# A state-space block with two mixers: u's second DFT and the transform back on mirrored rows, in 64x64 tiles

## Chip, cores, metric

One core of a Trainium2 chip runs the whole program in one launch. The metric is device time in microseconds (us) of that launch; lower is better. PE is the matmul engine, DVE the vector engine, ACT the scalar engine, POOL the general one, SP the engine that only issues DMAs and waits. Everything below is float32; a float32 matmul is two PE instructions in the trace, so counts of PE instructions there are twice the counts in the code.

## The reference

Shapes: A_u is [1, 2048, 512], the state has 128 complex modes for each of 512 channels.

```python
mod = (_silu(c) @ w_mod).reshape(c.shape[0], 6, 1, -1)
h = _layernorm(x) * (1 + ca) + sa
# _A_ref: K[d, l] = Re sum_n C[d,n] exp(dt A[d,n] l) dt B[d,n]; y = causal convolution of h with K
Kf = rfft(pad(K, 2L)); Uf = rfft(pad(h^T, 2L)); y = irfft(Uf * Kf)[:L] + h * Dskip
x = x + ga * y
h = _layernorm(x) * (1 + cb) + sb
x = x + gb * _B_ref(h)      # two LayerNorm/gelu mixers: shift by 1 and 2 rows between w1 and w2, then w3, w4
```

The part that changes is the convolution: the second step of the Fourier transform of `h` (called u here), the product with the spectrum of K, and the transform back.

## The kernel before

The program runs in three stages.

**Stage one (0 to 208 us).** It builds K by exponentials and sines, 32 rounds of `turns`, `products` and `burst`. Between the rounds it normalises u and does u's first DFT: a row number is 64q + b (q below 32, b below 64), and `u_dft` transforms over q by matmuls from 32 rows to 64 columns of the array (`FU`). Its results go out to DRAM (`VU`, by `evict`, one 64-partition DMA for each half of a tile).

**Stage two (208 to 322 us).** `k_first` (8 rounds) does the first DFT of K into `VK`. Then comes a loop of 16 steps: a step is a half of the channels (`jh`, 2) and four of the 32 first frequencies (`kc`, 8). A step has four parts:

- `spectrum_k` (line 669): second DFT of K over b, from `VK`, 32 matmuls with 64 rows and 64 columns each; result in two PSUM banks `pk2`.
- `multiply` (lines 680, 681, 685): on DVE, four products of 512 elements a partition and four sums and differences of 256; result `zc`.
- `back` (line 695): the first half of the inverse over `Gm`, 64 rows by 128 columns, real and imaginary part added up in PSUM (`pz`); ACT copies it to `z`, and POOL sends `z` to DRAM (`ZT`, line 701), 128 partitions of 4 KB.
- `spectrum_u` (line 646): second DFT of u over b and over real and imaginary part, 128 rows by 64 columns, with the weights `T2`; ACT copies the result to `us` in six pieces of 256.

The order in every engine's queue is the program's (`tc.manual_schedule()`): step n issues `spectrum_k(n)`, `multiply(n)`, `back(n-1)`, `spectrum_u(n+1)`, and then the loads. So PE runs K(n), back(n-1), U(n+1), K(n+1), and so on. `z`, `us` and `zc` have two buffers each: the copy into `z` of step n waits until the store of step n-2 has landed. `block` tiles (`ldp`, seven buffers) hold what SP loads: u's spectrum for step n+3, parts of w1, and what the second half of the inverse reads. SP's DMAs go out in program order, each waiting for the eighth before it to land; in steps 3, 4, 6 and 8 four DMAs each bring back the raw u (`load_x`, line 714, 32 partitions of 8 KB each, rows 128 KB apart in DRAM) for the residual.

The second half of the inverse, over k1 (`inv_half`, line 724), reads `ZT` back as [128, 4, 256] tiles (`load_inv`, line 709) and adds to the residual `X2` (line 727). It runs in eight groups (two channel halves by four groups g of four columns in each quarter). The first channel half's loads stand in the loop behind step 9 (g = 0), 13 and 14; its groups 0 and 1 are computed in the loop, groups 2 and 3 behind it. The second half's groups 3 and 0 come first behind the loop, since the mixers start from them.

**Stage three (322 to 705 us).** The two mixers, with weights split in a high and a low part (`three`, `chan`). The change does not touch them.

Of the kernel before, what the change touches and what calls it, by code (L numbers as in the profile page):

```python
# [21 lines left out]
JB = (1, 0, 2, 3)  # L22
# [5 lines left out]
def shape_constants():  # L28
# [5 lines left out]
    FU = np.zeros((4, 32, 2, 2, 2, 32))  # L34
    for h in range(2):
        for cp2 in range(2):
            cp = 2 * h + cp2
            FU[1 - cp if cp < 2 else cp, :, h, cp2] = W
    FU = FU.reshape(128, 2, 2, 2, 32).transpose(0, 1, 2, 4, 3)
# [6 lines left out]
    T3 = np.stack([s, -s]).reshape(128, 32 * 64)  # L46
    h, cq, cp2 = np.meshgrid(np.arange(2), np.arange(16), np.arange(2), indexing='ij')
    b = c2b((2 * h + cp2) * 16 + cq).reshape(64)
    al = 2 * np.pi * b[None, :] * k2[:, None] / 64
    c, s = np.cos(al), np.sin(al)  # L50
    Gm = np.zeros((64, 2, 64, 2))
    Gm[:, 0, :, 0], Gm[:, 0, :, 1], Gm[:, 1, :, 0], Gm[:, 1, :, 1] = c, s, -s, c
    Gm = np.tile(Gm.reshape(64, 256), (2, 1))
    FI = np.zeros((2, 2, 32, 16, 2, 2, 32))
    for hh in range(2):
        for c2 in range(2):
            for cc in range(16):
                bb = int(c2b(np.array((2 * hh + c2) * 16 + cc)))
                th = 2 * np.pi * (k1[:, None] + .5) * (bb + 64 * q[None]) / 4096
                FI[c2, 0, :, cc, hh, bb // 16 - 2 * hh] = np.cos(th) * (2 / 4096)  # L60
                FI[c2, 1, :, cc, hh, bb // 16 - 2 * hh] = -np.sin(th) * (2 / 4096)
# [19 lines left out]
    for e in range(16):  # L81
# [8 lines left out]
        FU=FU.reshape(128, 256), FK=FK.reshape(128, 128), T2=T2, T3=T3, G=Gm,  # L90
        FI=FI.reshape(128, 16 * 128), C0=C0, C1=C1, CE=CE, PA=PA.reshape(128, 512), PB=PB.reshape(128, 2048), ID=np.eye(128)).items()}


def layouts(inp):
    a = lambda n: np.asarray(inp[n])
    perm = lambda x: np.ascontiguousarray(x.reshape(4, 32, 4, -1).transpose(1, 0, 2, 3).reshape(512, -1))
    m = {"u": a("A_u")[0], "wm": a("w_mod"), "c": np.ascontiguousarray(a("c").reshape(4, 128).T),
         "ld": np.ascontiguousarray(perm(a("A_log_dt")).reshape(4, 128).T),
         "dk": a("A_Dskip").reshape(4, 128),
# [12 lines left out]
def body(ctx, tc, A):  # L112
# [76 lines left out]
    FU = ph.tile([128, 2, 128], F32, name="FU")  # L189
# [237 lines left out]
    def u_dft(b, cp2):  # L427
        x = ut[b // 4]
        ps = [psu.tile([128, 512], F32, name="pu") for h in range(2)]
        for i in range(2):  # L430
            for h in range(2):
                q = 64 * (1 - i if h == 0 else i)
                j = slice(32 * JB[2 * h + cp2], 32 * JB[2 * h + cp2] + 32)
                T.matmul(ps[h][q:q + 64], FU[j, h, cp2 * 64:cp2 * 64 + 64], x[j, b % 4 + i],  # L434
                         start=True, stop=True, skip_group_check=True)

        def evict():
            vs = uv.tile([128, 2, 512], F32, name="vs")
            for h in range(2):
                act(vs[:, h], ps[h])  # L440
                c0 = h * 32 + cp2 * 16 + (14 - b if h == 0 else b)
                for i in range(2):
                    Y.dma_start(dram(VU, (c0 + i) * 256, [[16384, 64], [1048576, 2], [1, 256]]),
                                vs[i * 64:i * 64 + 64, h].rearrange("p (a d) -> p a d", a=2))
# [158 lines left out]
    T3 = c2.tile([128, 32, 64], F32, name="T3")  # L603
    Gm = c2.tile([128, 2, 128], F32, name="Gm")
    FI = c2.tile([128, 16, 2, 64], F32, name="FI")
# [5 lines left out]
    psy = a2.enter_context(pool("psy", bufs=2, space=PSUM, side="right"))  # L611
    psa = s2x.enter_context(pool("psa", bufs=2, space=PSUM))
    BANK = ("pk1", "pk2", "pz", "py")
    block = lambda: ldp.tile([128, 4, 256], F32, name="ld")

    def k_first(r):
        ps = [(psy if n == "py" else psa).tile([128, 4, 2, 64], F32, name=n) for n in BANK]
# [20 lines left out]
    def spectrum_u(jh, kc):  # L638
        vu = vus.pop((jh, kc))
        us = s2.tile([128, 2, 3, 256], F32, name="us")  # L640
        for i in range(2):
            q = psa.tile([128, 2, 256], F32, name="pk1")
            for ro in range(2):
                for kk in range(2):
                    k1 = kc * 4 + 2 * kk + i
                    T.matmul(q[kk * 64:kk * 64 + 64, ro], T2[k1 // 16][:, k1 % 16, ro * 64:ro * 64 + 64],  # L646
                             vu[:, 2 * kk + i], start=True, stop=True, skip_group_check=True)
            for n in range(3):
                act(us[:, i, n].rearrange("p (h j g) -> p h j g", h=2, j=2),
                    q[:, n % 2].rearrange("p (j h g) -> p h j g", h=2, j=2))  # L650
        return us

    def spectrum_k(jh, kc):
        p = [psa.tile([128, 2, 2, 128], F32, name="pk2") for gh in range(2)]
        for i in range(2):
            for ro in range(2):
                for ri in range(2):
                    for kk in range(2):
                        for gh in range(2):
# [7 lines left out]
                            else:  # L667
                                w = T3[rows, k1]
# [5 lines left out]
    def multiply(jh, kc, us, p):  # L674
        zc = zcs[jh, kc] = [s2.tile([128, 2, 256], F32, name=f"zc{n}") for n in range(2)]
        m = []
        for gh in range(2):
            s = slice(gh * 128, gh * 128 + 128)
            m.append([s2.tile([128, 2, 2, 128], F32, name=n) for n in ("ma", "mb")])
            V.tensor_mul(m[gh][0], p[gh], us[:, :, :2, s])  # L680
            V.tensor_mul(m[gh][1], p[gh], us[:, :, 1:, s])
        as2 = lambda z: z.rearrange("p i (j g) -> p i j g", j=2)
# [612 lines left out]
```

## Time and profile before

| | |
|---|---|
| median of three runs | 707.08 us (704.25 to 710.23) |
| span of the profiled execution | 704.8 us; no other time is listed for it |
| PE busy | 666.8 us (95% of the span) |
| DVE, ACT, POOL busy | 500.4, 335.3 and 92.2 us |
| granted PE clock, mean | 0.996 of full speed |
| moved by DMA | 86.56 MB, mean 123 GB/s |

A page of the profile gives for each engine its busy time; a row of 40 digits, each the busy tenths of a slice of 17.6 us; then the chain of work that ended last, followed back from the last instruction, and groups of instructions with their mean duration. A matmul's duration includes its way through the array, and matmuls in different parts of the array overlap: what a group costs is read from the distance of its first and last start, not from the mean. "DMA share" in a table of stretches is the summed time of the packets over 16 DMA engines; 1.0 to 1.1 is all of them busy.

### The profile page before, as it was taken

Reading aid. Unit: us, or ns where it says so; the run is one execution under the profiler, and the core shown is the slowest. Engines: PE = TensorE matmul, PEld = TensorE weight load, DVE = VectorE, ACT = ScalarE, POOL = GpSimd, SP = SyncE. Lnnn points to the kernel's source line nnn. Section 1 sums busy time; section 2 is a strip of 40 time slices with the busy share of each in tenths; the row PEclk is TensorE's granted clock in tenths of the full one; section 3 lists DMA queues with packets and bytes.
Section 4 is the critical chain, followed back from the end, with each engine's and each line's share of the span. In section 5 each row is a group of like instructions: output and inputs, shape, how many; then the busy total and the mean of one; then the engine's idle time right before and its main releaser. Section 6 shows DMA issues by size and latency. Waiting matters only on the chain.

```text
span 704.8 us, 16806 instructions
## 1 busy us (share of the span) xinstructions
PE 666.8 (95%) x7067; PEld 516.0 (73%) x7067; DVE 500.4 (71%) x827; ACT 335.3 (48%) x553; POOL 92.2 (13%) x205
## 2 busy tenths in 40 slices
PE   1899999999999999998999899999999999999997
PEld 0456656565678565664778889899899988989896
DVE  7899999999986656778996867467455536354522
ACT  3978898888956354551443732224132221213120
POOL 4011121021100000001671101001110000000000
PEclk9999999999999999999999999999999999999999
DMA  8903274746449997885459111020110201011011
GB/s 289 285 2 93 78 210 125 181 103 189 134 125 340 233 276 266 293 278 201 144 185 301 61 31 31 16 56 21 55 36 16 66 11 39 22 30 31 1 31 31
DMA packets 56692, 86.56 MB, mean 123 GB/s; under 512 B 5541, under 2 KB 43433, under 8 KB 54921
## 3 DMA queue, kind: packets, MB, share of 16 engines
q1 hardware_dynamic: 52536, 66.87, 34.0%
q0 software_dynamic: 3200, 17.57, 7.0%
q8 instruction: 56, 0.92, 0.6%
q10 hardware_dynamic: 880, 1.05, 0.5%
q14 instruction: 20, 0.16, 0.1%
HBM read 59.25 MB, written 32.90 MB: 131 GB/s over the span
## 4 chain that ended last, share of the span: by engine, by line
PE 79%; DVE 11%; DMA 3%; ACT 3%; issue 2%; POOL 1%; SPq 0%; DVEq 0%; ACTq 0%; POOLq 0%
PE pm L834 7%; PE pm L831 7%; PE pm L832 7%; PE xx L457 7%; PE pa L947 6%; PE pa L948 6%; PE pa L955 6%; PE pk L669 4%; PE pk L646 4%; PE pz L695 4%; PE kp L507 4%; PE pu L434 2%; PE ph L886 2%; PE ph L888 2%; PE ph L885 2%; DMA w4l<-Dw 2%
## 5 line engine op out<-in xcount | busy, mean ns | idle before, releaser
L120 ACT ACTIVATE gh<-pm 128x512 fp32r<-128x512 f32 (+1 forms) x48 | 26.9, 561 | 200.7 <-PE pm L834 200.7
L831 PE MATMUL pm<-nh,w3h 128*128 128x256 f32 (+1 forms) x352 | 86.7, 281 | 2.9 <-ACT nh L120 2.9
L832 PE MATMUL pm<-nh,w3l 128*128 128x256 f32 (+1 forms) x352 | 86.3, 280 | 0.0
L939 DVE TENSOR_TENSOR gl<-gf,gh 128x512 fp32r<-128x512 f32 (+1 forms) x48 | 30.8, 642 | 68.3 <-ACT gf L120 68.3
L947 PE MATMUL pa<-w4h,gh 128*128 128x512 f32 (+1 forms) x176 | 69.5, 395 | 0.0
L831 PEld LDWEIGHTS pm<-nh,w3h 128*128 128x128 f32 (+1 forms) x352 | 66.0, 188 | 4.7 <-ACT nh L120 3.2
L948 PE MATMUL pa<-w4l,gh 128*128 128x512 f32 (+1 forms) x176 | 68.9, 391 | 0.0
L832 PEld LDWEIGHTS pm<-nh,w3l 128*128 128x128 f32 (+1 forms) x352 | 65.9, 187 | 1.8 <-DVE w3l L749 0.2
L834 PE MATMUL pm<-nl,w3h 128*128 128x256 f32 (+1 forms) x352 | 55.6, 280 | 0.0
L955 PE MATMUL pa<-w4h,gl 128*128 128x512 f32 (+1 forms) x176 | 48.0, 390 | 0.0
L834 PEld LDWEIGHTS pm<-nl,w3h 128*128 128x128 f32 (+1 forms) x352 | 47.4, 188 | 0.2 <-DVE nl L804 0.2
L758 POOL TENSOR_TENSOR rs<-mv,eps_t 128x1 f32<-128x1 f32 (+1 forms) x39 | 11.0, 282 | 278.5 <-DVE mv L764 265.9
L457 PE MATMUL xx<-MG,ON 64*128 64x512 f32 x160 | 47.0, 389 | 0.0
L458 PE MATMUL xx<-MG,ON 64*128 64x512 f32 x160 | 47.0, 389 | 0.0
L891 DVE TENSOR_TENSOR h<-h,ph 128x512 f32<-128x512 f32 x16 | 11.0, 687 | 45.4 <-PE ph L888 45.4
L475 DVE SCALAR_TENSOR_TENSOR e<-tr,p 128x512 f32<-128x512 f32 x64 | 41.1, 683 | 0.4 <-ACT tr L120 0.4
L120 ACT ACTIVATE z<-pz 128x512 f32<-128x512 f32 x32 | 17.4, 595 | 48.4 <-PE pz L695 17.1
L680 DVE TENSOR_TENSOR ma<-pk,us 128x512 f32<-128x512 f32 x32 | 21.9, 686 | 26.0 <-issue 11.8
L507 PEld LDWEIGHTS kp<-e,e 128*32 128x32 f32 x2048 | 30.1, 110 | 13.1 <-issue 7.1
L484 DVE TENSOR_TENSOR e<-tr,p 128x1024 f32<-128x1024 f32 x32 | 39.0, 1218 | 0.0
L485 DVE TENSOR_TENSOR e<-tr,m 128x1024 f32<-128x1024 f32 x32 | 39.0, 1218 | 0.0
L120 ACT ACTIVATE p<-xx 128x1024 f32<-128x1024 f32 (+1 forms) x40 | 37.5, 980 | 2.1 <-PE xx L258 0.4
(231 smaller groups left out, 1747.0 us busy)
## 6 DMA issues: line engine op xcount, KB each, us to landing
VU<-vs SPq DMA_DIRECT2D x64, 128.0 KB, 3.2
ld<-VU SPq DMA_DIRECT2D x16, 512.0 KB, 15.1
ZT<-z POOLq DMA_DIRECT2D x15, 512.0 KB, 6.9
ld<-ZT SPq DMA_DIRECT2D x12, 512.0 KB, 7.0
Dw<-in_w POOLq DMA_DIRECT2D x8, 688.0 KB, 4.8
xu<-in_u SPq DMA_DIRECT2D x16, 256.0 KB, 10.2
KX<-in_u SPq DMA_DIRECT2D x16, 256.0 KB, 13.2
GD<-go SPq DMA_DIRECT2D x16, 256.0 KB, 2.2
```

Of the source, the lines that this page charges most:

```text
L120: return S.activation(out, in_, f, bias=bias, scale=scale)
L457: T.matmul(x[:, :512], la, ma, start=(i == 0), stop=(i == len(ops) - 1))
L458: T.matmul(x[:, 512:], lb, mb, start=(i == 0), stop=(i == len(ops) - 1))
L475: V.scalar_tensor_tensor(e0[:, 1, a], tr[:, 1, 0], 1.0 - 2.0 * a, mg[:, a], op0=OP.mult, op1=OP.mult)
L484: V.tensor_mul(e0[:, 0], tr[:, 0, 0:1].to_broadcast([128, 2, 512]), mg)
L507: T.matmul(kp[32 * j:32 * j + 32, (k % 2) * 4 + g], e1[:, r, d], e0[:, r, :, d * 32:d * 32 + 32], start=(r == 0), stop=(r == 1), skip_grou ...
L831: T.matmul(p, wh[:, k, c], hi[k], start=(k == 0), stop=False)
L832: T.matmul(p, wl[:, k, c], hi[k], start=False, stop=False)
L834: T.matmul(p, wh[:, k, c], lo[k], start=False, stop=(k == 3))
L947: T.matmul(acc[i], gh[:m, e, s], W4h[:m, f], start=(f == 0), stop=False)
L948: T.matmul(acc[i], gh[:m, e, s], W4l[:m, f], start=False, stop=False)
L955: T.matmul(acc[i], gl[:m, e, s], W4h[:m, f], start=False, stop=(f == 10))
```

## The change

The block of 64 columns b is taken as 32 pairs mirrored about its middle (31 - b' and 32 + b'). `u_dft` now forms sums and differences within its matmuls: its rows hold both columns of a pair and its weights hold W and W with the order turned round and its sign. Each call makes one kind (`eo`), from 64 rows to 64 columns of the array. With them the real and the imaginary part of the second DFT need 64 rows each, so `spectrum_u` contracts over 64 rows with the new weights `TU`, and `back` gives the cosine and the sine product of each part apart (`Gm` is half as large, no adding up in PSUM). The signs of a pair's two members are then in `FI`, and `inv_half` makes 32 rows of one column at a time.

```diff
 def load_u(g):
-    for bp in range(4):
-        Y.dma_start(x[bp * 32:(bp + 1) * 32],
-                    dram(A["u"], (bp * 16 + g * 4) * 512, [[64 * 512, 32], [1, 2048]]))
+    for n, bp in enumerate(UB):                                    # UB = (1, 2, 0, 3)
+        Y.dma_start(x[n * 32:(n + 1) * 32],
+                    dram(A["u"], (bp * 16 + g * 4) * 512, [[64 * 512, 32], [1, 2048]]) if bp > 1 else
+                    dram(A["u"], (bp * 16 + 15 - g * 4) * 512, [[64 * 512, 32], [-512, 4], [1, 512]]))
 def u_dft(b, eo):
-            j = slice(32 * JB[2 * h + cp2], 32 * JB[2 * h + cp2] + 32)
-            T.matmul(ps[h][q:q + 64], FU[j, h, cp2 * 64:cp2 * 64 + 64], x[j, b % 4 + i], ...)
+            j = slice(64 * h, 64 * h + 64)
+            T.matmul(ps[h][i * 64:i * 64 + 64], FU[j, eo], x[j, b % 4 + i], ...)
-psy = a2.enter_context(pool("psy", bufs=2, space=PSUM, side="right"))
 psa = s2x.enter_context(pool("psa", bufs=2, space=PSUM))          # pk1, pz (before: pk2 too)
+psb = s2x.enter_context(pool("psb", bufs=4, space=PSUM))          # pk2: four banks instead of two
 def spectrum_u(jh, kc):
-    us = s2.tile([128, 2, 3, 256], F32, name="us")
-    for i in range(2):
-        q = psa.tile([128, 2, 256], F32, name="pk1")
-        for ro in range(2):
-            for kk in range(2):
-                k1 = kc * 4 + 2 * kk + i
-                T.matmul(q[kk * 64:kk * 64 + 64, ro], T2[k1 // 16][:, k1 % 16, ro * 64:ro * 64 + 64],
-                         vu[:, 2 * kk + i], start=True, stop=True, skip_group_check=True)
-        for n in range(3):
-            act(us[:, i, n].rearrange(...), q[:, n % 2].rearrange(...))
+    us = s2.tile([128, 3, 2, 256], F32, name="us")
+    q = [psa.tile([128, 2, 256], F32, name="pk1") for ro in range(2)]
+    for i in range(2):
+        for kk in range(2):
+            for ro in range(2):
+                r = slice(ro * 64, ro * 64 + 64)
+                T.matmul(q[ro][kk * 64:kk * 64 + 64, i], TU[r, kc * 4 + 2 * kk + i], vu[r, 2 * kk + i],
+                         start=True, stop=True, skip_group_check=True)
+    for n in range(3):
+        act(us[:, n], q[n % 2])
+def flip(kc):                       # the T3, formerly loaded by two DMAs, from T2
+    t = t3s[kc] = c2.tile([128, 8, 64], F32, name="T3", bufs=3)
+    for gh in range(2):
+        r = slice(gh * 64, gh * 64 + 64)
+        P.tensor_scalar(t[r], T2[kc // 4][r, kc % 4 * 4:kc % 4 * 4 + 8, 64 - gh * 64:128 - gh * 64], -1.0, None, op0=OP.mult)
 def multiply(jh, kc, us, p):
-    m = []
-    for gh in range(2):
-        s = slice(gh * 128, gh * 128 + 128)
-        m.append([s2.tile([128, 2, 2, 128], F32, name=n) for n in ("ma", "mb")])
-        V.tensor_mul(m[gh][0], p[gh], us[:, :, :2, s])
-        V.tensor_mul(m[gh][1], p[gh], us[:, :, 1:, s])
-    for gh in range(2):
-        for n in range(2):
-            V.tensor_tensor(zc[n]..., as2(m[gh][n][:, :, 0]), as2(m[gh][n][:, :, 1]), op=(OP.subtract, OP.add)[n])
+    m = [s2.tile([128, 2, 2, 2, 128], F32, name=n, bufs=1) for n in ("ma", "mb")]
+    for gh in range(2):
+        for n in range(2):
+            V.tensor_mul(m[n][:, gh], p[gh], us[:, n:n + 2, :, gh * 128:gh * 128 + 128].rearrange("p r i d -> p i r d"))
+    for n in range(2):
+        V.tensor_tensor(zc[n]..., m[n][:, :, :, 0], m[n][:, :, :, 1], op=(OP.subtract, OP.add)[n])
 def back(jh, kc):
-            T.matmul(o[kk], Gm[r, n], zc[n][r], start=(n == 0), stop=(n == 1))
+            T.matmul(o[kk][n * 64:n * 64 + 64], Gm[r, n], zc[n][r], start=True, stop=True, skip_group_check=True)
+    def store(q, a, b):
+        for n in range(2):
+            q.dma_start(dram(ZT[jh], n * 16384 + (kc * 4 + a) * 256, [[32768, 32], [8192, 2], [1, (b - a) * 256]]),
+                        z[n * 64:n * 64 + 64, a:b].rearrange("p k d -> p (k d)"))
-        P.dma_start(ZT[jh][:, kc * 4:kc * 4 + 4], z)
+        store(P, 0, 4)
 def inv_half(jh, g, i, pl, name):
-        for h in range(2):
-            T.matmul(p[h * 64:h * 64 + 64, e], FI[:, cc, h], zz[h][:, cc % 4], ...)
+        for bp, (c, sg) in enumerate(((31 - b, 1), (15 - b, 1), (b, 0), (16 + b, 0))):
+            T.matmul(p[bp * 32:bp * 32 + 32, e], FI[:, c, sg], zis[jh, c // 4][:, c % 4], ...)
 # in the loop
+            if n % 2 == 0 and n < 14:
+                flip(steps[n + 2][1])
-            if n == 9: load_inv(0, 0)
+            if n == 10:
+                for k in (0, 3, 4, 7): load_inv(0, k)
-            if n == 11: inverse(0, 0)
+            if n == 12: inverse(0, 0)
-            if n == 13: load_inv(0, 1); load_inv(0, 2)
-            if n == 14: load_inv(0, 3)
+            if n == 13:
+                inverse(0, 3)
+                for k in (1, 2, 5, 6): load_inv(0, k)
 # behind the loop
-    inverse(0, 2)
-    inverse(0, 3)
+    for i in range(2):
+        inv_half(0, 2, i, psy, "py")()
```

Three places show how the queues move. The first is SP's queue from step 8 of the loop on; L636 and L626 are the loads of u's spectrum, L743 and L738 those of w1 and then w2, L709 and L707 those of the inverse (`ld<-ZT`), `FI` its weights. Before:

```order
40 L743 DMA ld<-in_w 128x2x512
41 L636 DMA ld<-VU 128x4x256
42 L1127 DMA FI<-in_FI 128x2048
43 L743 DMA ld<-in_w 128x2x512
44 L709 DMA ld<-ZT_61 128x4x256 x2
45 L636 DMA ld<-VU 128x4x256 x3
46 L743 DMA w2l<-Dw_64 128x2x512 x2
47 L709 DMA ld<-ZT_61 128x4x256 x6
48 L699 DMA ZT_62<-z 128x512
```

And with the change:

```order
53 L738 DMA ld<-in_w 128x2x512
54 L626 DMA ld<-VU 128x4x256
55 L1125 DMA FI<-in_FI 128x2048
56 L738 DMA ld<-in_w 128x2x512
57 L626 DMA ld<-VU 128x4x256
58 L707 DMA ld<-ZT_61 128x4x256 x4
59 L626 DMA ld<-VU 128x4x256 x2
60 L738 DMA w2l<-Dw_64 128x2x512 x2
61 L707 DMA ld<-ZT_61 128x4x256 x4
62 L692 DMA ZT_62<-z 32x2x512 x2
```

The first loads of the inverse stand behind one more load of u's spectrum and are four instead of two; the other four (before six) follow w2.

The second place is POOL's queue in the loop: the issues of the stores of `z`, and with the change `flip` (L648) between them. Before:

```order
59 L521 DMA Dw_64<-in_w 16x8192 x2
60 L701 DMA ZT_61<-z 128x1024 x8
61 L701 DMA ZT_62<-z 128x1024 x7
62 L758 TENSOR_TENSOR rs_79<-mv_78,eps_t 128x1
```

With the change:

```order
59 L510 DMA Dw_64<-in_w 16x8192 x2
60 L648 TENSOR_SCALAR T_3093<-xu 64x512 x2
61 L648 TENSOR_SCALAR T_3368<-xu 64x512 x2
62 L692 DMA ZT_61<-z 32x2x1024 x4
63 L648 TENSOR_SCALAR T_3514<-xu 64x512 x2
64 L692 DMA ZT_61<-z 32x2x1024 x4
65 L648 TENSOR_SCALAR T_3663<-xu 64x512 x2
```

A step's store is two DMAs of 64 partitions instead of one of 128, and every second step a pair of `flip` instructions stands behind them.

The third is DVE in a step in the middle of the loop: products into `ma` and `mb`, then sums and differences into `zc`. Before:

```order
323 L680 TENSOR_TENSOR ma<-pk_3938,us 128x512
324 L681 TENSOR_TENSOR mb<-pk_3938,us 128x512
325 L680 TENSOR_TENSOR ma<-pk_3939,us 128x512
326 L681 TENSOR_TENSOR mb<-pk_3939,us 128x512
327 L685 TENSOR_TENSOR zc_3972<-ma 128x4x64
328 L685 TENSOR_TENSOR zc_3973<-mb 128x4x64
329 L685 TENSOR_TENSOR zc_3972<-ma 128x4x64
330 L685 TENSOR_TENSOR zc_3973<-mb 128x4x64
```

With the change:

```order
327 L676 TENSOR_TENSOR ma<-pk_4145,us 128x512
328 L676 TENSOR_TENSOR mb<-pk_4145,us 128x512
329 L676 TENSOR_TENSOR ma<-pk_4146,us 128x512
330 L676 TENSOR_TENSOR mb<-pk_4146,us 128x512
331 L678 TENSOR_TENSOR zc_4179<-ma 128x2x2x128
332 L678 TENSOR_TENSOR zc_4180<-mb 128x2x2x128
```

Four short instructions have become two of twice the length.

More of the change, by code (lines that the diff above doesn't have):

```diff
@@ L33, in shape_constants @@
     W = np.stack([np.cos(th), -np.sin(th)], 1)
-    FU = np.zeros((4, 32, 2, 2, 2, 32))
-    for h in range(2):
[L36 to L39, printed above, removed]
+    Wt = W.transpose(0, 2, 1)
+    FU = np.stack([np.stack([Wt, -Wt[..., ::-1]], 1), np.stack([Wt, Wt[..., ::-1]], 1)])
+    FU = np.stack([FU, FU])
     FK = np.zeros((2, 2, 32, 2, 64))
@@ L717, in inv_half @@
     def inv_half(jh, g, i, pl, name):
-        zz = zis[jh, g]
         p = pl.tile([128, 2, 256], F32, name=name)
         for e in range(2):
-            for h in range(2):
-                b = g * 4 + i * 2 + e
-                cc = 15 - b if h == 0 else b
-                T.matmul(p[h * 64:h * 64 + 64, e], FI[:, cc, h], zz[h][:, cc % 4],
+            b = g * 4 + i * 2 + e
+            for bp, (c, sg) in enumerate(((31 - b, 1), (15 - b, 1), (b, 0), (16 + b, 0))):
+                T.matmul(p[bp * 32:bp * 32 + 32, e], FI[:, c, sg], zis[jh, c // 4][:, c % 4],
                          start=True, stop=True, skip_group_check=True)
@@ L727, in inv_half, with inverse_parts @@
         return lambda: V.tensor_add(x, p, x)
-    def inverse_parts(jh, g):
-        return [inv_half(jh, g, i, psy, "py") for i in range(2)]
+    def inverse_parts(jh, g, pl, name):
+        return [inv_half(jh, g, i, pl, name) for i in range(2)]
     def inverse(jh, g):
-        for f in inverse_parts(jh, g):
+        for f in inverse_parts(jh, g, psa, "pz"):
             f()
@@ L1114, in body @@
             if n == 15:
-                i1 = inverse_parts(0, 1)
+                i1 = inverse_parts(0, 1, psb, "pk2")
             if n < 15:
@@ L1157, in body @@
         psw = ctx.enter_context(tp("psw", 2, space=PSUM))
+        psy = a2.enter_context(tp("psy", 2, space=PSUM, side="right"))
         def keep(n):
```

125 lines of the change are left out of this document (57 added, 68 removed).

## The prediction

> **What bounds the kernel now.** First the page: which engine is busy, and where.
>
> ```profile
> span 704.8 us, 16806 instructions
> ...
> PE 666.8 (95%) x7067; PEld 516.0 (73%) x7067; DVE 500.4 (71%) x827; ACT 335.3 (48%) x553; POOL 92.2 (13%) x205
> ...
> DMA  8903274746449997885459111020110201011011
> ```
>
> PE is the bound of the whole, but the change lies in stage two, slices 12 to 18, and there the DMA row reads 9998788: nearly as full as PE. So two limits have to be weighed. The chain of waits, cut to a quiet stretch of the loop, shows the first:
>
> ```profile
> 278.45 1.91 PE pk L669 x64
> 280.36 1.92 PE pz L695 x8
> 282.28 1.88 PE pk L646 x16
> 284.16 1.91 PE pk L669 x64
> ```
>
> K, back and U follow each other with no gap: a step is 284.16 - 278.45 = 5.71 us, all PE. The second limit stands in a table of four stretches of the loop:
>
> ```profile
> 224.80:273.50 48.70, 46.87 (x727) 29.14 (x729) 30.59 (x64) 21.19 (x63) 3.39 (x7) 1.00 1.06 279
> 273.50:286.00 12.50, 12.50 (x221) 7.89 (x214) 7.95 (x17) 7.65 (x23) 1.44 (x3) 1.00 0.38 132
> 286.00:310.00 24.00, 24.00 (x359) 14.72 (x359) 20.09 (x42) 12.40 (x35) 2.12 (x4) 1.00 1.02 356
> 310.00:322.40 12.40, 11.73 (x144) 6.36 (x136) 10.29 (x21) 5.94 (x14) 1.06 (x2) 1.00 0.46 156
> ```
>
> The last three columns are granted clock, DMA share and GB/s. For 72.7 of 97.6 us the sixteen DMA engines are full, at two very different rates. And the waits in the loop:
>
> ```profile
> ACT z L120 <- DMA ZT<-z: 13.2, 3, 5.7
> ...
> DVE ma L680 <- ACT us L120: 9.8, 4, 4.0
> ```
>
> Three times ACT could not overwrite `z` because the store two steps back had not landed; what stands behind it in ACT's queue (the copies to `us`) then held DVE. The DMAs already touch the chain.
>
> **The change part by part: PE.** The rows of the three matmuls, with rows by columns of the array in use and the size of one:
>
> ```profile
> L669 PE MATMUL pk<-VK,xu x768: 266/269/321, 224.8 to 316.0; 64*64 64x128 f32 x192
> L646 PE MATMUL pk<-ld,xu x256: 379/379/431, 223.0 to 314.0; 128*64 128x256 f32 x128
> ...
> L695 PE MATMUL pz<-zc,Gm x128: 589/589/693, 231.5 to 322.2; 64*128 64x512 f32 x128
> ```
>
> K streams 64 instructions of 128 columns in 1.91 us, U 16 of 256 in 1.88, back 8 of 512 in 1.92: 8192 columns and 4096 twice, in the same time, because K's quarters of the array run four at a time and the halves of the others two. The change makes U and back quarters with the same number of instructions and columns, so I give them K's rate: 0.94 and 0.96 us. A step becomes 1.91 + 0.94 + 0.96 = **3.8 us**, 1.9 less, 30 us over 16 steps. The sharing between the array's quarters is bounded by K's row (1.9 saved) and by no gain at all (0).
>
> **DVE and ACT.** One step's instructions, as starts:
>
> ```profile
> 318.35 0.68 DVE L680 TENSOR_TENSOR ma<-pk,us 128x512 f32<-128x512 f32 x1
> ...
> 319.54 0.41 DVE L685 TENSOR_TENSOR zc<-ma 128x256 f32<-128x256 f32 x1
> 319.87 0.42 DVE L685 TENSOR_TENSOR zc<-mb 128x256 f32<-128x256 f32 x1
> ...
> L120 ACT ACTIVATE us<-pk 128x256 f32<-128x256 f32 x94 | 27.8, 399 | 2.4 <-PE pk L646 2.0 <-ACT z L120 0.4
> ...
> L120 ACT ACTIVATE z<-pz 128x512 f32<-128x512 f32 x30 | 16.3, 595 | 46.0 <-PE pz L695 17.1 <-DMA ZT<-z 13.2 <-issue 10.5
> ```
>
> A product comes every (319.54 - 318.35) / 2 = 0.60 us, a short sum every 0.33: 4 x 0.60 + 4 x 0.33 = 3.7 us now, 6 x 0.60 = 3.6 with two long ones. ACT: 6 x 27.8/94 + 2 x 16.3/30 = 2.9 now, 5 x 0.54 = 2.7 then. So DVE and PE come level at 3.6 to 3.8 us; the four `pk2` banks let K(n+1) run beside multiply(n), which two banks did not allow. By the engines a step could fall to about 3.9 us.
>
> **DMA, the term that decides.** What is moved in the loop stays the same (`TU` is as large as the old `T3`). Full engines read 1.02 to 1.06, so the loop's transfers alone need (48.70 x 1.06 + 12.50 x 0.38 + 24.00 x 1.02 + 12.40 x 0.46) / 1.06 = 86.6 / 1.06 = **81.7 us**, and of 97.6 us at most 15.9 can go. Some of it stays: behind the last loads only stores are left, and there is nothing to fill about one step and a half. I take 5 us as idle (the stretch from 310 has 54% of 12.4, or 6.7 us). That leaves **-11 us** for the loop. Its ends are -16 (nothing idle) and -4 (as idle as now, 12 us).
>
> The stretch at 279 GB/s is slow by its loads of raw u, and that bears on the stores, which the change cuts in two halves of 64 partitions:
>
> ```profile
> 21.00:25.00 4.00, 3.89 (x10) 3.04 (x10) 3.96 (x4) 3.79 (x7) 0.00 (x0) 1.00 1.06 394
> 26.00:34.00 8.00, 7.35 (x46) 3.79 (x38) 5.28 (x9) 6.96 (x11) 0.00 (x0) 1.00 1.01 218
> 64.40:65.00 0.60, 0.60 (x34) 0.45 (x36) 0.60 (x2) 0.53 (x2) 0.00 (x0) 1.00 0.94 195
> ...
> ZT<-z POOLq DMA_DIRECT2D x15, 512.0 KB, 6.9
> ...
> ZT<-z POOLq DMA_DIRECT2D x1, 512.0 KB, 3.0
> ```
>
> The first stretch loads `w_mod` to 128 partitions, the second u to 32 partitions at a time, the third stores `VU` from 64: 394, 218 and 195 GB/s with the engines equally full. (Their steps in DRAM differ too, so the rows alone don't say which of the two it is.) A store of 512 KB is 1.3 us at the first rate and 2.5 at the others: the halves cost between 0 and 1.2 us more each. Stores that go out beside the u loads meet a slow queue anyway; of the eight behind them some meet 128-partition loads, which keep the engines busy while a half-store waits. I take +1 us in all, nearest to none, and keep 0 and +10 (eight stores in full) as ends. The two last rows are the median time to land, in the loop and once with nothing beside it.
>
> [...]
>
> **POOL and SP.**
>
> ```profile
> 266.63 0.37 SPq L743 DMA_DIRECT2D ld<-in_w  x1
> 283.58 0.92 SPq L709 DMA_DIRECT2D ld<-ZT  x2
> ...
> 248.98 0.53 POOL L701 DMA_DIRECT2D ZT<-z  x1 [7.88 <-ACT z L120]
> ...
> 262.13 0.53 POOL L701 DMA_DIRECT2D ZT<-z  x1 [7.93 <-ACT z L120]
> ...
> 278.03 0.53 POOL L701 DMA_DIRECT2D ZT<-z  x1 [4.16 <-ACT z L120]
> 283.74 0.53 POOL L701 DMA_DIRECT2D ZT<-z  x1 [5.17 <-ACT z L120]
> ...
> L853 POOL COPY win<-go x2: 501/502/504, 355.8 to 359.4; 128x384 f32<-128x384 f32 x2
> ```
>
> POOL issues a store in 0.53 us; two make 1.1. `flip` is new: 16 instructions of 64 x 512. The nearest row is 0.50 us for 384 elements a partition, so 0.7 each, 1.3 a pair and 11 us in all, bounded by 0 and twice that; POOL has 3.39 of 48.70 us busy, so it fits between stores. A new wait comes of it: K(n+2) waits for the flip, which stands behind the store of step n-1, whose copy waits for a landing. It has two steps' time; if that cover is gone it costs up to 2.4 us in a step.
>
> SP sat from 267.0 to 283.6 until the store of step 7 (issued 278.03) had landed, with all later loads behind it. The change puts one more load of u ahead of that wait and needs 2 MB instead of 1 before the first inverse in step 12; at the 356 GB/s above that is 3 us more on a wait that two steps cover. I take 0, the end is +4.
>
> **Stage one.** u's first DFT keeps its count and sizes:
>
> ```profile
> L434 PE MATMUL pu<-xu,FU x128: 587/613/638, 61.3 to 202.5; 32*64 32x512 f32 x128
> ...
> L147 DVE BATCH_NORM_STATS2 lus<-xu x16: 662/687/689, 39.8 to 179.0; 128x6 f32<-128x512 f32 x16
> ```
>
> It used four parts of the array before (two of rows, two of columns) and does after: 0, with ends of -1 and +1. Half of u's loads come in 2 KB pieces; the first loads are over at 34 us, u is first read at 39.8: the six us between cover them.
>
> **Behind the loop.**
>
> ```profile
> 326.39 3.68 DMA ld<-ZT
> ...
> 330.20 1.10 PE py L724 x8
> ```
>
> The first inverse of the second half waited 3.7 us for 512 KB. It now needs four tiles' halves, 1 MB: 0.5 MB at 356 GB/s is +1.5. The last `back` is 0.96 shorter, the second piece of the last store is issued 0.37 later (SP's row above): **+0.9**. The inverse's own matmuls are twice as many with half the columns of the array, four side by side for two: 0. One group of four fewer remains here, in time in which PE waited; one more is in the loop, where PE is no longer the bound.
>
> **Sum:** -11 + 1 + 0.9 = -9 against the span, 695.7. The median of the three runs stands 2.3 us above the span, so 698 is what I expect of a median.
>
> **The rivals.**
>
> *The engines are the bound (12%).* The DMA share shrinks with less competition, and DVE sets the steps.
>
> ```profile
> L749 DVE TENSOR_TENSOR w1l<-ld,w1h 128x512 fp32r<-128x512 f32 x4 | 2.6, 688 | 2.1 <-ACT w1h L120 2.1
> ```
>
> Eight steps at 3.9 are 31; the other eight 8 x 3.6 with the splits of w1 and (taken alike) w2, 2 x 2.6, and four additions of an inverse, 4 x 0.6: 37. With a last step run out, 3.8, that is 72 for 97.6, -26. Against it: a share of 1.06 for 48.7 us. Time 707 - 26, about 682.
>
> *What the loop gains is lost to late landings (33%).* Half-stores pay for the eight steps (+10), or the first inverse stalls PE (+4) and the last steps idle as now (+7). The loop ends where it did: 704 to 709, and 707 stands for it.
>
> *Slower (7%).* The half-stores pay 1.2 us each in all 15 stores, since engines that wait for one can do nothing else: 81.7 + 5 + 18 = 105 us for 97.6, +7, with the tail +8: 715. It decides from the ninth store that pays in full (81.7 + 5 + 9 x 1.2 = 97.5). For it: 195 GB/s in the one pure half-store row; against it: the loop's stores never run alone.
>
> *PE's clock drops in the new gaps (8%).* It has happened in this trace:
>
> ```profile
> 389.97 0.39 PE L831 MATMUL pm<-nh,w3h 128*128 128x256 f32 x1 [2.94 <-ACT nh L120]
> ...
> 391.30:394.80 3.50, 3.50 (x18) 3.39 (x17) 3.47 (x7) 1.18 (x4) 0.00 (x0) 0.51 0.36 111
> ```
>
> After 2.94 us of waiting PE ran 3.5 us at 0.51, a loss of 1.7 us of matmul time. Amid the u loads two steps took 262.13 - 248.98 = 13.15 us by POOL's stores, 6.6 each; of such a step PE would now wait 6.6 - 3.8 = 2.8; seven such drops are 7 x 1.7 = 12 us of PE time, a third of it perhaps on the path: +4, time 702. [...]
>
> *The quarters don't overlap (2%).* U and back then keep their time: 707. K's row speaks against it.
>
> **Numbers.** The forecast has 38%, its own range 691 to 703 (loop -16 to -4, less or more of the +1). **The range 686 to 709** leaves out the engine-bound case and the slower one. One per cent, 7 us, is about what a measurement of this kernel can tell from no change: faster than 700.0 is two thirds of the forecast, the engine-bound case and a fourth of the clock and late cases, **0.48**; slower than 714.2 **0.07**; the rest **0.45**.
>
> **What would show it.** Right: L636 and L688 (U and back) at 0.94 and 0.96 us a step; DMA share about 1.05 without the dip at 273 to 286; z's copies waiting for `ZT` landings more than 13.2 us; the loop from 225 to 310 or 312. Wrong: a share well under 1 with steps of 3.9 us (engines), stores landing 3 us later than 6.9 (halves), a clock column under 0.9 in the loop, or PE waiting for `ld<-ZT` in step 12.

## The result, and the profile after

The changed kernel took 699.33 us (median of 12 runs, 697.88 to 705.2) against 705.89 of the kernel before on the same chip (703.27 to 710.84): a ratio of 0.9922, with a 95% interval of 0.9893 to 0.9951, so 3.5 to 7.6 us faster. Its profiled execution has a span of 699.7 us, 5.1 less than before. The page's rows that answer to those of before:

```profile
span 699.7 us, 16980 instructions
...
PE 639.1 (91%) x7195; PEld 507.1 (72%) x7195; DVE 497.8 (71%) x795; ACT 331.9 (47%) x505; POOL 125.3 (18%) x236
...
DMA  8903274745539999987268111020110201011011
```

PE worked 27.7 us less and the program ended 5.1 us sooner: most of what was taken off PE turned into waiting. The table of the four stretches of the loop (busy time of PE, PE's weight loads, DVE, ACT and POOL, then granted clock, DMA share and GB/s) says where:

```profile
224.80:273.50 48.70, 35.07 (x740) 27.12 (x732) 29.77 (x49) 20.47 (x40) 17.10 (x20) 0.89 1.06 277
273.50:286.00 12.50, 10.85 (x261) 9.05 (x255) 10.59 (x19) 8.99 (x19) 6.85 (x9) 1.00 0.78 251
286.00:310.00 24.00, 20.70 (x424) 14.21 (x424) 23.21 (x41) 13.04 (x27) 10.10 (x12) 1.00 1.03 353
310.00:322.40 12.40, 7.17 (x78) 3.24 (x78) 8.55 (x17) 2.16 (x5) 1.07 (x2) 0.99 0.50 136
```

In the first stretch PE is busy for 35.07 us instead of 46.87, at the same share (1.06) and the same rate (277 for 279 GB/s). POOL's issues of stores are the loop's milestones: the first, the eighth (step 7) and the fifteenth. Of the kernel before (the eighth, 278.03, stands in the prediction), then of the changed one:

```profile
235.11 0.57 POOL L701 DMA_DIRECT2D ZT<-z  x1 [52.55 <-ACT z L120]
...
319.68 0.53 POOL L701 DMA_DIRECT2D ZT<-z  x1 [5.17 <-ACT z L120]
```

```profile
232.05 1.19 POOL L692 DMA_DIRECT2D ZT<-z  x2 [13.38 <-ACT z L110]
...
275.23 1.07 POOL L692 DMA_DIRECT2D ZT<-z  x2 [1.76 <-ACT z L110]
...
310.32 1.07 POOL L692 DMA_DIRECT2D ZT<-z  x2 [2.97 <-ACT z L110]
```

From the first store to the eighth it took 42.9 us before and 43.2 now; from the eighth to the fifteenth 41.7 before and 35.1 now. The gain at the fifteenth is 9.4 us: 3.1 stood there at the first store, none came in the seven steps amid the loads of raw u, 6.6 behind them.

The chain of waits shows a kind of wait in the first half that the kernel before hardly had (rows with start, length and what it was):

```profile
231.50 1.74 issue
...
238.03 5.68 issue
...
251.01 1.17 issue
...
257.18 2.13 issue
...
267.07 2.43 issue
...
302.04 1.91 PE pk L666 x64
303.95 0.86 PE pz L688 x8
304.81 0.86 PE pk L636 x16
```

The three last rows are K, back and U in a quiet step: 3.63 us for what took 5.71 (the next K follows at 305.67). The five others are PE in the middle of a group, waiting for no semaphore that the profile shows. What the waits add up to, and behind it PE's wait on K in the kernel before:

```profile
DVE ma L676 <- PE pk L666: 17.0, 8, 6.4
...
ACT z L110 <- DMA ZT<-z: 13.0, 3, 5.3
...
PE pk L666 <- issue: 10.7, 6, 5.7
```

```profile
PE pk L669 <- issue: 1.3, 2, 0.7
```

And behind the loop, where the last step's products lead to the last piece of the last store, and this to the loads of the inverse. Two rows of the kernel before, then the chain of the changed one:

```profile
317.15 0.68 DVE L680 TENSOR_TENSOR ma<-pk,us 128x512 f32<-128x512 f32 x1
...
323.92 0.35 ACTq L699 DMA_DIRECT2D ZT<-z  x1
```

```profile
309.30 0.60 DVE ma L676
...
316.18 2.85 DMA ZT<-z
...
319.84 4.95 DMA ld<-ZT
...
324.93 1.97 PE py L719 x16
```

The first inverse of the second half starts at 324.93 instead of 330.20, 5.3 us sooner: of the 9.4 us, 4.1 were given back in the tail. From there to the end it is 374.8 us now and 374.6 before.

### The profile page after: what moved, and what is told of

Same layout as the page of the kernel before. It is cut to its first block, busy times and chain, and to the rows that moved or that the text cites. A ratio compares the mean times of both kernels' runs of the same rounds, so it can differ in the third digit from the quotient of the medians.

```text
span 699.7 us, 16980 instructions
## 1 busy us (share of the span) xinstructions
PE 639.1 (91%) x7195; PEld 507.1 (72%) x7195; DVE 497.8 (71%) x795; ACT 331.9 (47%) x505; POOL 125.3 (18%) x236
## 3 DMA queue, kind: packets, MB, share of 16 engines
q10 hardware_dynamic: 896, 1.05, 0.6%
## 4 chain that ended last, share of the span: by engine, by line
PE 69%; DVE 17%; issue 4%; DMA 4%; ACT 3%; POOL 1%; SPq 0%; ACTq 0%; DVEq 0%; POOLq 0%
PE pm L829 7%; PE pm L827 7%; PE pm L826 7%; PE pa L950 6%; PE pa L942 6%; PE pa L943 6%; PE xx L446 6%; PE pk L666 3%; PE kp L496 3%; PE pz L688 2%; DVE e L464 2%; DVE e L474 2%; PE pk L612 2%; PE ph L881 2%; PE ph L883 2%
## 5 line engine op out<-in xcount | busy, mean ns | idle before, releaser
L666 PE MATMUL pk<-VK,xu 64*64 64x128 f32 x768 | 36.8, 274 | 10.7 <-issue 10.7
L666 PEld LDWEIGHTS pk<-VK,xu 64*64 64x64 f32 x768 | 32.7, 135 | 14.0 <-issue 13.2
L950 PEld LDWEIGHTS pa<-w4h,gl 128*128 128x128 f32 (+1 forms) x176 | 33.0, 188 | 8.3 <-DVE gl L934 1.2
```

The costliest lines, as they stand in the source:

```text
L666: T.matmul(p[gh][kk * 64:kk * 64 + 64, i, ro], w, VK[jh][rows, ri * 32 + k1].rearrange("p j g -> p (j g)"), start=(ri == 0), stop=(ri == 1 ...
L950: T.matmul(acc[i], gl[:m, e, s], W4h[:m, f], start=False, stop=(f == 10))
```

## The experiments

All are variants of the changed kernel unless said otherwise; ratios are against the kernel before, run beside them. Milestones in us from the profiled executions:

| | store 1 | store 8 | store 15 | first inverse behind | span | ratio (95%) |
|---|---|---|---|---|---|---|
| before | 235.11 | 278.03 | 319.68 | 330.20 | 704.8 | |
| changed | 232.05 | 275.23 | 310.32 | 324.93 | 699.7 | 0.9922 (0.9893 to 0.9951) |
| changed, again | 232.60 | 278.12 | 313.72 | 328.32 | 702.7 | 0.9926 (0.9906 to 0.9946) |
| old tiles | 233.95 | 276.45 | 320.93 | 334.60 | 709.3 | 1.0087 (1.0058 to 1.0116) |
| half the code of K | 232.09 | 272.01 | 307.30 | 321.57 | 696.5 | 0.9929 (0.9906 to 0.9952) |
| whole stores | 232.12 | 271.71 | 306.78 | 319.30 | 693.8 | 0.9897 (0.9865 to 0.9928) |
| no raw u | 232.72 | 261.65 | 295.93 | 310.26 | 685.7 | 0.9751 (0.9710 to 0.9792) |
| raw u to 128 partitions | 231.65 | 263.89 | 296.61 | 312.05 | 686.7 | 0.9764 (0.9742 to 0.9786) |
| before, raw u to 128 | 235.25 | 274.97 | 316.62 | 326.67 | 701.8 | 0.9965 (0.9952 to 0.9978) |
| raw u copied first | 232.14 | 264.17 | 298.70 | 312.85 | 687.7 | 0.9775 (0.9756 to 0.9795) |

The row "again" is the changed kernel, run beside two other kernels of this section:

> The changed kernel unaltered, as the measure for its neighbours on the same chip: 0.989 to 0.995 of the kernel before.

It gave 0.9926. Its profiled execution was 3 us longer than the first one, all of it within the loop, so a difference of 3 us between two single profiles of kernels with slow loads proves nothing by itself. Its fifteenth store came 6.0 us sooner than in the kernel before, where the first profile had 9.4; the tail, 14.6 us from there to the first inverse, is the same in both.

**Old tiles: is PE's saving worth anything?**

```diff
-                    T.matmul(q[ro][kk * 64:kk * 64 + 64, i], TU[r, kc * 4 + 2 * kk + i], vu[r, 2 * kk + i],
+                    T.matmul(q[ro][kk * 64:kk * 64 + 64, i], TU[:, kc * 4 + 2 * kk + i], vu[:, 2 * kk + i],
...
-                T.matmul(o[kk][n * 64:n * 64 + 64], Gm[r, n], zc[n][r], start=True, stop=True, skip_group_check=True)
+                T.matmul(o[kk], Gm[r].rearrange("p n m -> p (n m)"), zc[n][r], start=(n == 0), stop=(n == 1))
```

> U and back are given the old tiles again (U 128 rows by 64 columns, back 64 rows by 128 columns, in the same number of instructions; the values are not those of the reference), all else as in the changed kernel: 1.88 and 1.92 us instead of 0.86 to 0.96 each. If the transfers alone set the loop, the time stays within 2 us of 699. If PE sets a part of it (steps 9 to 15, where PE is busy without a gap from 292 to 307): 6 or 7 steps by 1.9 us later, 9 to 13 us slower than the changed kernel, that is slower than the kernel before by 3 to 7 us.

It took 710.42 us. Against the changed kernel's ratio that is 1.0087 - 0.9922 = 0.0165, or 11.6 us: the quarters of the array are worth as much as the whole loop term of the prediction, and the rest of the change costs 6 us. The milestones split it: to the eighth store the old tiles lose 1.2 us, from there to the fifteenth 44.5 - 35.1 = 9.4. PE's saving counts only in the second half.

**Half the code: are PE's stalls the bound of the first half?**

```diff
-                            T.matmul(p[gh][kk * 64:kk * 64 + 64, i, ro], w, VK[jh][rows, ri * 32 + k1]...)
+                            # once for both ro
+                            T.matmul(p[gh][kk * 64:kk * 64 + 64, i], w, VK[jh][rows]...[:, :, k1], ...)   # 256 columns
```

> K's second DFT gives PE the same 4096 columns a step in 16 matmuls of 256 columns instead of 32 of 128 (its values are no longer those of K), so a step has 112 PE instructions instead of 176 and nothing else changes. Theory 1, PE waits for its own code: the five stalls of the changed kernel at 231.5, 238.0, 251.0, 257.2 and 267.1 (13.2 us together) stand 253 to 254 matmuls and weight loads apart and end 1.5 us behind a 16 KB packet of the instruction queue; with 112 instructions a step a block lasts 2.3 steps, or over 8.5 us, so the stalls shrink to under 4 us in all, step 7's store goes out 3 to 8 us earlier and the time falls by 2 to 6 us. Theory 2, the transfers set the loop and the stalls lie beside them: PE's stalls turn into waits of ACT for landings of ZT, step 7's store goes out within 1 us of 280.7, and the time stays within 2 us of the changed kernel's 699.

699.54 us, ratio 0.9929: no gain that the runs can tell. The five stalls are gone: with 112 instead of 176 instructions a step the waits have no row of PE on K for `issue`, where it was 10.7 us, so PE waited for its code. What stands in their place in this kernel's chain of waits:

```profile
232.72 10.41 DMA ZT<-z
...
245.25 9.69 DMA ZT<-z
...
257.01 10.24 DMA ZT<-z
```

ACT can't overwrite `z` until a store has landed, 10 us later, three times. The eighth store went out 3.2 us sooner in this profile, on the low side of what theory 1 asked, and the runs' times side with theory 2. Both waits are for transfers of the same full engines (a share of 1.06 up to 273.5 us in both kernels): the 10.7 us on K went, and ACT's waits for landings grew from 13.0 to 18.3 us.

**Whole stores: what do the halves cost?**

```diff
-            for n in range(2):
-                q.dma_start(dram(ZT[jh], n * 16384 + (kc * 4 + a) * 256, [[32768, 32], [8192, 2], [1, (b - a) * 256]]),
-                            z[n * 64:n * 64 + 64, a:b]...)
+            q.dma_start(dram(ZT[jh], (kc * 4 + a) * 256, [[8192, 128], [1, (b - a) * 256]]), z[:, a:b]...)
```

> Each step's z goes out in one DMA of 128 partitions instead of two of 64, to rows 32 KB apart as before (the rows land in another order, so what the inverse reads is permuted). If halves cost what the single half-stores suggest (1.2 us each in the steps where the engines wait for them): stores land 1 us sooner and the time falls by 2 to 8 us. If other transfers fill the engines beside a half-store: within 2 us of the changed kernel's 699, gaining only POOL's 0.53 us of issue in a step and the tail's two issues, at most 1 us.

697.44 us. By the ratios 0.9922 - 0.9897 = 0.0025, 1.8 us, with intervals that overlap; the profile alone would say 5.9. From the fifteenth store to the first inverse it took 12.5 us instead of 14.6, so part of it lies in the tail. The halves cost between nothing and some 5 us, which holds the +1 of the prediction; the runs don't settle it more closely.

**No raw u in the loop.**

```diff
-            if n in (3, 4, 6, 8):
-                load_x(n - 3 if n < 5 else n // 2 - 1)
```

> The raw u (4 MB in 16 DMAs of 32 partitions) is not brought back in the loop, so the residual is missing and the loop's transfers lose what ran at about 215 GB/s, some 19 us of full engines. Theory 1, the transfers hold the first half of the loop (through late landings of ZT and late blocks of PE's code, both of which queue behind the loads): the eight first steps take 4 to 4.5 us instead of 6.3, the loop ends 12 to 18 us sooner, time 682 to 688. Theory 2, the engines' own chain (DVE 3.6 us, ACT, two buffers of z) holds it as it is: at most 5 us sooner, time 694 to 700.

687.29 us. The first seven steps take 28.9 us instead of 43.2, or 4.1 each. Theory 1 held: it is those 4 MB.

**What makes them slow: the 32 partitions or the rows 128 KB apart?** Two kernels change one thing and both.

```diff
-            Y.dma_start(X2[bp * 32:(bp + 1) * 32, ...], dram(A["u"], (bp * 16 + g * 4) * 512, [[64 * 512, 32], [512, 4], [1, 512]]))
+            # pitch alone: 32 KB
+            Y.dma_start(X2[bp * 32:(bp + 1) * 32, ...], dram(A["u"], (bp * 32 * 16 + g * 4) * 512, [[16 * 512, 32], [512, 4], [1, 512]]))
+        # both: one DMA of 128 partitions for a group
+        Y.dma_start(X2[:, g * 4:g * 4 + 4]..., dram(A["u"], g * 4 * 512, [[16 * 512, 128], [1, 2048]]))
```

> As the run with 128 partitions, but in sixteen DMAs of 32 partitions as in the changed kernel: of its loads only the pitch in DRAM differs, 32 KB instead of 128. If the pitch is what makes the loads slow: as fast as with 128 partitions (8 KB packets near 309 ns, time 690 to 696). If it is the 32 partitions: 8 KB packets stay at 540 to 650 ns and the time within 2 us of the changed kernel's 699.

> The raw u comes in four DMAs of 128 partitions, whose 8 KB rows lie 32 KB apart (other rows of u than the residual needs; the bytes are the same). If both the partitions reached and the pitch are cured by it: the loads run at 350 to 390 GB/s, the stretch from 225 to 273 shows over 330 GB/s or ends 8 us sooner, time 690 to 696. If neither matters: 277 GB/s and 699.

The pitch alone gave 700.66 us (0.9934, 0.9911 to 0.9957), the 128 partitions 688.66. What moved from 225 to 258 us, in the changed kernel, with the other pitch, and with 128 partitions:

```profile
DMA packets 4387, 8.45 MB, mean 256 GB/s; under 512 B 400, under 2 KB 3496, under 8 KB 3998
```

```profile
DMA packets 4957, 9.53 MB, mean 289 GB/s; under 512 B 455, under 2 KB 3929, under 8 KB 4536
```

```profile
DMA packets 6168, 13.00 MB, mean 394 GB/s; under 512 B 392, under 2 KB 4495, under 8 KB 5535
```

The engines are full in all three (the queues' shares add up to 107%, 107% and 104%). A packet of 8 KB took 590, 512 and 313 ns (medians from 224 to 258 us; in the first two kernels `FI`, which has such packets too, is loaded later). Whether the pitch has a share is not shown, for half the code of K, with the changed kernel's own loads, had 513. The large step is the one to 128 partitions, and only it shows in the time. It also makes four DMAs of 1 MB out of sixteen of 256 KB; no run separates the two, but it is the single packet that takes less time, by a factor of 590 / 313 = 1.9. What makes it so is not shown. The table of stretches with 128 partitions:

```profile
224.80:273.50 48.70, 44.09 (x982) 34.32 (x976) 41.57 (x68) 28.86 (x57) 23.37 (x29) 1.00 0.96 346
273.50:286.00 12.50, 11.71 (x232) 8.15 (x228) 12.39 (x23) 6.21 (x13) 8.18 (x8) 1.00 1.06 381
```

DVE works 41.57 of 48.70 us and 12.39 of 12.50, PE's clock stays at 1.00, and PE's waits for instructions shrink to 1.2 us on K:

```profile
PE pk L666 <- issue: 1.2, 2, 0.8
```

So DVE is near its bound, as in the rival "the engines are the bound", though a step takes 4.6 us here ((263.89 - 231.65) / 7) and the rival had 3.9. Note that from 225 to 258 the engines were nearly as full here as there (the queues' shares add up to 104% and 107%); with packets of 313 ns a half-store issued there landed in 6.8 us (median) and PE waited 1.2 us for instructions on K, with packets of 590 it was 10.3 and 10.7.

**The kernel before with the same fast loads.** The same edit in the kernel before:

> The kernel before with the raw u in four DMAs of 128 partitions with rows 32 KB apart (other rows than the residual needs), as the changed kernel had them in the run at 688.7. If PE's step of 5.71 us bounds the kernel before: PE stood idle for only 1.8 us of 224.8 to 273.5 and 0.7 of 310 to 322.4, so 1 to 4 us faster than before, 701 to 705, and the change would be worth 13 us where loads are fast. If slow loads bounded the kernel before as well: 6 to 12 us faster, 693 to 699, and the change is worth as much as with slow loads.

703.44 us, 0.9965, 2.5 us faster; its stores go out every 5.70 us. So the change takes the kernel from 0.9965 to 0.9764 where loads are fast, 14.3 us of 705 (1.0 - 0.9764 / 0.9965 = 2.0%), and from 1 to 0.9922, 5.5 us, where they are slow. The difference of 9 us is what the slow loads took of its gain.

**Three ways of loading that failed.** One DMA for four groups of 32, with the right rows:

```diff
-        for bp in range(4):
-            Y.dma_start(X2[bp * 32:(bp + 1) * 32, ...], ...)
+        Y.dma_start(X2[:, g * 4:g * 4 + 4]..., dram(A["u"], g * 4 * 512, [[16 * 512, 4], [64 * 512, 32], [1, 2048]]))
```

> Each group of four DMAs of 32 partitions that bring the raw u back becomes one DMA of 128 partitions with the same rows, 8 KB packets and addresses in DRAM. [...]

724.93 us, 1.029 (1.0265 to 1.0316), the slowest of all these kernels. In its first stretches the engines were not even full:

```profile
235.00:245.00 10.00, 7.13 (x172) 6.03 (x165) 6.76 (x12) 3.20 (x7) 4.26 (x4) 1.00 0.55 167
245.00:273.50 28.50, 23.83 (x448) 16.48 (x448) 18.56 (x31) 14.57 (x29) 12.50 (x16) 0.94 0.66 211
```

The addresses in DRAM have 4 as their slowest dimension, and from 235 to 273 us hardly ever more than four of its 8 KB packets were under way at once (for 1% of the time), where the changed kernel had up to 14; the share is 0.55 to 0.66. The four loads of 128 partitions above (688.66 us) differ from these in their addresses in DRAM alone; which of their properties makes the difference is not shown. So this run says nothing about partitions.

Half of the loads from POOL's queue, to the other 64 partitions:

```diff
-                load_x(n - 3 if n < 5 else n // 2 - 1)
+                load_x(n - 3 if n < 5 else n // 2 - 1, Y, (0, 1))
+            if n in (0, 1, 3, 5):
+                load_x((n + 1) // 2, P, (2, 3))
```

> The same sixteen loads of raw u as in the changed kernel, but those to partitions 64 to 127 go out from POOL's queue (steps 0, 1, 3 and 5) and those to partitions 0 to 63 from SP's, so that the engines have packets for both halves in hand. If the rate hangs on how many partitions are being written at a time: the stretch from 225 to 273 shows over 300 GB/s or ends 5 us sooner, PE's stalls for code shrink, time 690 to 696. If each transfer of 32 partitions is slow by itself: 277 GB/s and 697 to 701. If the stores of z, which stand behind these loads in POOL's queue, land later and hold ACT: 701 to 707.

701.95 us, 0.9958 (0.9929 to 0.9987): no better than one queue, perhaps worse, with PE's waits for instructions hardly smaller (9.5 us on K for 10.7), 540 ns a packet (to 258 us) and 292 GB/s in the first stretch, short of the 300 that the first theory asked. Why two queues to different partitions are no faster is open.

Two of the four groups later:

```diff
-            if n in (3, 4, 6, 8):
-                load_x(n - 3 if n < 5 else n // 2 - 1)
+            if n in (3, 6):
+                load_x(n - 3)
...
+                load_x(1)     # behind the inverse's loads in step 10
...
+                load_x(2)     # the same in step 13
```

> The same bytes, but the two groups of raw u that the first inverse groups don't need are loaded behind the inverse's loads of steps 10 and 13 instead of in steps 4 and 8 (group 3 moves from step 8 to step 6), where the engines showed a share of 0.69 (280 to 286) and 0.47 (310 to 315). If transfers set the first half and the later share is idle time that can be filled: the first half ends 6 to 9 us sooner, some 3 of it are given back later, time 693 to 697. If the later half is as full as the first: within 2 us of the changed kernel. If the late loads get in the way of the last stores and the first loads behind the loop: 2 to 5 us slower than the changed kernel.

702.16 us, 0.9963 (0.9936 to 0.9989). The eighth store went out at 267.36, 7.9 us sooner, the fifteenth at 305.30 and the first inverse came at 324.21: in this profile the gain was given back, 2.9 us in the second half and 4.3 in the tail. By the ratios it is 2.9 us slower than the changed kernel, with intervals that overlap: on the side of the third theory.

**The right rows, fast.** A version that computes what the reference asks for and loads to 128 partitions: raw u is first copied within DRAM, at a time when the engines are idle, into the order of the residual.

```diff
+    US = [dpool.tile([128, 2048], F32, name=f"US{g}") for g in range(4)]
...
+        for g in range(4):                      # behind load_u(1), in stage one
+            for bp in range(4):
+                Y.dma_start(US[g][bp * 32:bp * 32 + 32], dram(A["u"], (bp * 16 + g * 4) * 512, [[64 * 512, 32], [1, 2048]]))
...
     def load_x(g):
-        for bp in range(4):
-            Y.dma_start(X2[bp * 32:(bp + 1) * 32, ...], ...)
+        Y.dma_start(X2[:, g * 4:g * 4 + 4].rearrange("p b d -> p (b d)"), US[g])
```

> The changed kernel, with the raw u copied once within DRAM into the order of the residual's partitions (sixteen DMAs behind the first loads of u, where the engines showed a share of 0.01 from 44 to 57 us), so that the loop brings it back in four DMAs of 128 partitions, now the right rows. If the 32 partitions are what costs and the copies find idle engines: the loop as in the run at 688.7, time 688 to 693, 0.976 to 0.983 of the kernel before. If the copies hold up the stores of u's first DFT or PE's code in stage one by as much as they save: 695 to 701.

689.82 us (688.75 to 690.71), 0.9775 of the kernel before and 10 us better than the change alone. The copies move 8 MB, read and written, while the engines had next to nothing to do, and the loop is that of the 128 partitions (share 0.96, 346 GB/s in its first stretch).

## Why the prediction was right, point by point

It said 698 with a range of 686 to 709; 699.33 was measured, and -9 against the span stands beside -5.1 in the profile and 5.5 (3.5 to 7.6) in the runs. The time came nearer than the gain, and some of that is luck: 698 was counted from three runs with a median of 707.08, and twelve gave 705.89.

- **The loop, -11 and +1 for the halves: right in size.** The fifteenth store came 9.4 us sooner in the first profile, 6.0 in the second. It is right that the full engines decide, not PE's 30 us: without the raw u, or with it to 128 partitions, the fifteenth store comes at 296 to 297, 23 us sooner than before.
- **The same, its picture: right for the idle time, silent on what else decides.** The sum took the loop's transfers as a block of 81.7 us that is filled more tightly. Added up in the same way, the changed kernel has (48.70 x 1.06 + 12.50 x 0.78 + 24.00 x 1.03) / 1.06 = 81.2 us of full engines in the 85.2 up to 310. The stretch that was full stayed as it was: the eighth store moved by 2.8 us only, and while raw u was loaded the steps took as long as before. The gain came behind it, where a share of 0.38 became 0.78 and where PE and DVE set the steps: old tiles cost 9.4 us there. But 81.7 us is no fixed amount. With raw u to 128 partitions the same bytes took the engines less time (313 ns for a packet of 8 KB instead of 590), and the first steps fell to 4.6 us where they had been 6.2 (43.2 over seven).
- **PE: right.** U and back took 0.86 us each in a quiet step, 0.94 and 0.96 were forecast; K stayed at 1.91.
- **The tail, +0.9: the term that was mis-sized.** It cost 4.1 us: the last piece goes out 316.18 - 310.32 = 5.9 us behind the fifteenth store instead of 323.92 - 319.68 = 4.2, takes 2.8 instead of 2.3 to land, and from the first load behind it to the inverse it is 324.93 - 319.23 = 5.7 instead of 330.20 - 326.24 = 4.0. The sum had seen the larger loads (+1.5; +1.7 came), not the later last piece, +1.6 where -0.6 was reckoned. DVE is the late one now: the last step's products start at 309.22 (the chain joins them at 309.30), 1.1 us ahead of the fifteenth store, where it was 2.5 before (317.15). And ACT's second half goes out 0.96 us behind its first (315.22), where 0.37 was reckoned. In the profile with whole stores 2.1 of the 4.1 us were gone: there the halves cost more in the tail than the sum's whole +1.
- **POOL: the size was wrong, the conclusion right.** A `flip` took 1.54 us, not 0.7, within the bound of twice that:

```profile
L648 POOL TENSOR_SCALAR T<-xu 64x512 f32<-64x512 f32 x12 | 18.5, 1543 | 0.9
```

PE waited 0.4 us for it in all; the two steps of cover were enough. Where the steps are shorter, with raw u to 128 partitions, they were not quite: PE waited 2.7 us for `flip`, in four waits.
- **z's copies waiting more than 13.2 us for landings:** 13.0 in the first profile, 18.4 in the second, where PE waited less for its code (6.7 us on K for 10.7), and 18.3 with half the code. The two waits stand in for each other.
- **The clock rival** came true without deciding: the granted clock was 0.89 in the first stretch (0.77 from 235 to 245, around the stall of 5.68 us). PE had 13 us to spare there. No run takes the drops away by themselves, so their price is open.
- **The dip at 273 to 286 and late landings:** the dip was filled in part only (a share of 0.78 where 1.05 was forecast). The stores landed in 6.8 us (median) for 6.9, and no first inverse waited in step 12, so the late-landings rival did not come; half-stores cost between nothing and 5 us.
- **The engine-bound rival** had the time of a kernel that was not run then: 682 with DVE at the bound, 688.7 with raw u to 128 partitions.
- **Stage one, 0: right.** The first U of the loop starts at 222.95 us, 223.0 before.
- **A misreading:** the prediction quotes slices 12 to 18 of the DMA row as 9998788; counted from 0, as it seems to do, they read 9997885. No term of the sum hangs on it.

## What to carry to other kernels

Full DMA engines at two rates are two different limits: raw u, which nobody waits for in the loop, held up stores and PE's own instructions with packets of 590 ns (10.3 us to land, 10.7 us of waits on K), and far less with 313 ns (6.8 and 1.2). Beside the slow packets the saving on the busiest engine only moved the wait. Before an engine is relieved, look at what it will wait for next, and mend that first or with it: here the same change was worth 5.5 us beside loads to 32 partitions and 14.3 beside loads to 128. And follow a gain to the point where the next stage starts, for here a tail with more, smaller transfers gave 4.1 of 9.4 us back.

## What the runs showed of the hardware

- PE's instructions come through the same DMA engines, and were late five times (13.2 us together). In the changed kernel the five stalls lie 252 to 254 matmuls and weight loads apart. In the stretch from 225 to 273 us the queue of instructions moved:

```profile
q8 instruction: 5, 0.08, 0.8%
```

five packets of 16 KB, and each of the five stalls ends 1.4 to 1.6 us behind the end of one of them. The kernel before moved the same five there and waited 1.3 us on K: its PE was busy for 46.87 us with about as many matmuls (727 records, 740 with the change), instead of for 35.07. With 112 instead of 176 instructions in a step the stalls were gone; with the same code and raw u to 128 partitions they fell from 10.7 us on K to 1.2, though the engines were nearly as full.
- 128 partitions instead of 32 in a load, and 1 MB instead of 256 KB: 313 ns instead of 590 for a packet of 8 KB, and runs that lie closer together (four from 688.5 to 689.0, where twelve of the changed kernel lie between 697.9 and 705.2).
- One load of 1 MB whose addresses in DRAM go in 4 steps of 32 rows cost 26 us by the ratios (1.029 for 0.9922) against four of 256 KB with the same rows: but for 1% of the time no more than four of its 8 KB packets were under way at once, where the changed kernel had up to 14.
